# A fused attention and GEGLU kernel: weights loaded ahead of q and v of batch 1, the first GEGLU ahead of its q part, the first output projection beside batches 1 and 2, v weighted on GpSimd

## Chip, cores, metric

One core of one Trainium2 chip. The metric is the device time of one execution in microseconds; smaller is better. Runs of the kernel before and of a variant alternate on the same chip.

## The reference, cut to what matters

```python
# q, k, v: 8 batches x 8 heads x 576 x 64; omega: 128 x 64
def phi(x):                       # x is already scaled
    h = einsum('bhsd,md->bhsm', x, omega) - sum(x*x)/2
    return exp(h - max(h, over m)) / sqrt(128)
q_p, k_p = phi(q), phi(k)
kv, z = einsum('bhsm,bhsd->bhmd', k_p, v), sum(k_p, over s)
x = (q_p @ kv) / (q_p @ z + 1e-6)          # 4608 tokens x 512
out = (gelu(x @ w_gate) * (x @ w_val)) @ w_out     # d_ff = 1536
```

For each batch of attention the kernel transposes k and q, takes exp of the projected keys (k_p), their maxima (from which a weight wk for each row of v), v times wk, the products kz of keys and v, the exp of the projected queries, and the numerators and denominators (nd), whose quotient x is transposed. Nine token tiles of 512 rows then go through GEGLU (12 gates, 12 vals) and the output projection (48 matmuls each). In steady state the attention of batch t+1 runs beside the projection of tile t-1 and the GEGLU of tile t.

## The kernel before: the parts that matter

```python
att = PSUM pool, bufs=2 (two banks each);  mo = PSUM pool, bufs=4 (one bank each)
ld  = SBUF pool, bufs=2 (k_in, q_in, vf);  work = SBUF pool, bufs=2

load_kq("k", 0, parts=2); load_kq("q", 0); load_v(0)       # DMAs issued by GpSimd
load_kq("q", 1); load_kq("k", 1); load_gv(0); load_v(1)    # load_gv: 512 columns of gate and val
load_gv(1); load_gv(2); load_kq("k", 2); load_kq("q", 2)
# ... three loads of w_out, then load_v(2)

def transposed_dma(nm, b):        # used from batch 2 on; issued on the SyncE queue
    t_sb = work.tile([P, NI, P], BF16, name=f"{nm}T", tag="kqT")
    nc.sync.dma_start_transpose(out=t_sb, in_=loaded.pop((nm, b)))

def v_half(self, half):
    nc.vector.tensor_mul(ve[half], vf[half], wk[half])     # 128 x 1152
    nc.vector.tensor_copy(ve[half, D], wk[half])

def start():                      # batches 0 and 1, GEGLU 0; the issue order of each engine
    kp(0, dve); kp(1, act)        # transposed on TensorE in four pieces, copied out
    a.k_chunk(0); a.k_chunk(1); kp(2, act); kp(3, dve)
    a.k_chunk(2); a.k_chunk(3); qp(0, act); qp(1, dve)
    a.k_chunk(4); qp(2, act); qp(3, dve); a.weights()
    a.q_chunk(0); a.v_half(0); a.q_chunk(1); a.v_half(1)
    a.q_chunk(2); a.kz(0)
    # ... q chunks, nd and x of batch 0 interleaved with q of batch 1 (transposes, q chunks), k of batch 1
    g = Gated(0); g.gate(0); n.k_chunk(2); g.val(0); n.k_chunk(3); g.gate(1); n.k_chunk(4)
    n.weights(); g.gelu(0); g.mul(0); n.v_half(0); g.gelu(1); g.val(1); g.mul(1); n.v_half(1)
    for jf in range(2, 12):
        g.both(jf)                # gate, gelu, val, mul
        # jf 3: n.kz(); jf 4 to 8: n.nd; jf 5 to 9: n.xt; jf 5 and 9: transposed_dma of k and q of batch 2

def step(t, before):              # t = 1, 2, ...
    p = Projection(t - 1, before.gated); a = Attention(t + 1)
    begun = a.k_pair(0); load_batch(t + 2, begun)
    p.go(15); a.k_pair(2); p.go(13)                # go(n): n projection matmuls
    a.k_chunk(4); a.q_chunk(0); a.weights(); a.v_half(0)
    p.go(11); a.q_chunk(1); a.q_chunk(2); a.v_half(1); p.go(9)
    # ... gate 0, last q chunks, gelu 0, val 0, both(1), kz, then GEGLU with nd of the batch
```

Some names in the code: `kp(i, engine)` and `qp(i, engine)` transpose piece i of k or q on TensorE and copy it out on the engine named. `k_chunk(c)` projects one of five chunks of keys, takes its exp on ScalarE and its maxima on VectorE; `k_pair(c)` does two chunks crosswise: ScalarE begins with one and VectorE with the other. `q_chunk(c)` projects queries and takes their exp. `nd(i)` makes numerators, denominators and their quotient, `xt(i)` transposes that quotient. A PSUM buffer holds the result of matmuls until other engines have read it.

The softmax here doesn't subtract the row's maximum and nothing guards it: scores larger than these inputs give would overflow.

## Time and profile before

| kernel before | |
|---|---|
| median of the first three runs (lowest to highest) | 360.52 us (359.94 to 363.45) |
| span of the profiled execution, TensorE busy | 358.9 us, 338.2 us |
| TensorE idle from 5 to 60 us | 11.5 us (55 less the busy times of those windows) |
| TensorE idle from 60 to 340 us | 3.1 us, in part matmul records that the trace lacks (it shows 3 of the 4 of the first gate below) |

The lines below are from the overview: the span and the rows of 40 slices of about 9 us, with each digit the busy tenths of a slice. PEclk is the granted TensorE clock in tenths.

```profile
span 358.9 us, 6528 instructions
...
PE   6786997999999999999999999999999999999994
...
DVE  3986884747475747584758475757665334323431
ACT  4897324563457246623763366436643113303310
...
PEclk9899999999999999999999999999999999999999
```

The sum of busy times is in the table. TensorE is full from the eighth slice on. As long as it stays full there, relief of another engine is worth nothing; what idle time can be won lies in the first 60 us (another 4.7 us lie at the very end, after 340 us, which the change leaves alone). The next lines are windows of that stretch (start:end and length, then busy us and number of instructions for PE, PEld, DVE, ACT and POOL, and last the granted clock, the DMA share and GB/s).

```profile
core 0: us, PE busy (x) PEld busy (x) DVE busy (x) ACT busy (x) POOL busy (x), PEclk, DMA share, GB/s
10.00:15.00 5.00, 4.08 (x34) 2.43 (x34) 4.73 (x8) 4.50 (x8) 1.49 (x2) 0.66 1.11 309
15.00:20.00 5.00, 4.34 (x107) 2.95 (x107) 4.44 (x11) 4.90 (x12) 1.01 (x2) 1.00 1.22 208
20.00:25.00 5.00, 4.26 (x61) 2.84 (x59) 4.45 (x17) 4.99 (x11) 1.51 (x3) 1.00 1.19 282
...
55.00:60.00 5.00, 2.53 (x14) 0.98 (x12) 1.38 (x2) 2.45 (x3) 0.00 (x0) 1.00 1.25 146
66.00:80.00 14.00, 13.79 (x140) 6.29 (x141) 8.23 (x12) 9.20 (x17) 0.00 (x0) 1.00 1.02 257
80.00:90.00 10.00, 9.95 (x81) 5.05 (x79) 7.37 (x15) 2.99 (x5) 0.00 (x0) 1.00 0.30 61
```

ScalarE and VectorE are nearly full from 10 to 25 us, so it is they that set the pace there. From 55 to 60 TensorE is busy half of the time. The timeline of TensorE names the causes (start, duration, instruction, and in brackets the idle time before it and what ended it):

```profile
27.51 1.04 PE L325 MATMUL g_ps<-xT,w_gate_sb 128*128 128x512 bf16 x3
...
36.05 1.02 PE L325 MATMUL g_ps<-xT,w_gate_sb 128*128 128x512 bf16 x4 [2.91 <-ACT g_gelu L331]
...
60.00 0.62 PE L204 MATMUL pk<-omegaT_124,kT 64*128 64x128 bf16 x16 [2.47 <-DMA kT<-k_in]
```

GEGLU 0 starts at 27.51. Its third gate waits 2.91 us for the first GELU, which ScalarE's timeline shows behind one table load:

```profile
33.87 0.23 ACT L234 ACTIVATE wk<-nmax 128x36 f32<-128x36 f32 x1 [1.06 <-DVE nmax L214]
34.11 1.28 ACT L331 ACT_TABLE_LOAD   x1
35.40 1.09 ACT L331 ACTIVATE g_gelu<-g_ps 128x512 bf16<-128x512 f32 x2
```

The last wait, 2.47 us, is for the DMA transpose of k of batch 2. On SyncE's queue its issue alone takes 11.87 us (start, duration), and the chain of waits (the second line) gives it 18.86 us until it lands; it starts as soon as k has landed, with q and v of batch 2 and w_out still loading:

```profile
41.09 11.87 SPq L157 DMA_TRANSPOSE kT<-k_in  x1
...
41.09 18.86 DMA kT<-k_in
```

### The profile page before, as it was taken

Reading aid. Unit: us, or ns where it says so; the run is one execution under the profiler, and the core shown is the slowest. Engines: PE = TensorE matmul, PEld = TensorE weight load, DVE = VectorE, ACT = ScalarE, POOL = GpSimd, SP = SyncE. Lnnn points to the kernel's source line nnn. Section 1 sums busy time; section 2 is a strip of 40 time slices with the busy share of each in tenths; the row PEclk is TensorE's granted clock in tenths of the full one; section 3 lists DMA queues with packets and bytes.
Section 4 is the critical chain, followed back from the end, with each engine's and each line's share of the span. In section 5 each row is a group of like instructions: output and inputs, shape, how many; then the busy total and the mean of one; then the engine's idle time right before and its main releaser. Section 6 shows DMA issues by size and latency. Waiting matters only on the chain.

```text
span 358.9 us, 6528 instructions
## 1 busy us (share of the span) xinstructions
PE 338.2 (94%) x2653; PEld 164.1 (46%) x2694; DVE 207.4 (58%) x337; ACT 162.6 (45%) x260; POOL 26.1 (7%) x40
## 2 busy tenths in 40 slices
PE   6786997999999999999999999999999999999994
PEld 3552553454444544454445443544354444444443
DVE  3986884747475747584758475757665334323431
ACT  4897324563457246623763366436643113303310
POOL 8222001100020002000200020000000000000000
PEclk9899999999999999999999999999999999999999
DMA  8999999983289257944593439561312040031013
GB/s 121 270 272 208 207 214 166 220 229 66 68 148 299 58 76 114 317 63 90 85 311 82 102 50 315 115 104 29 76 22 58 21 98 0 1 74 45 0 31 90
DMA packets 64399, 44.12 MB, mean 123 GB/s; under 512 B 44784, under 2 KB 57840, under 8 KB 64368
## 3 DMA queue, kind: packets, MB, share of 16 engines
q0 software_dynamic: 15392, 23.60, 31.3%
q1 hardware_dynamic: 48816, 19.97, 26.2%
q8 instruction: 21, 0.34, 0.4%
q10 hardware_dynamic: 160, 0.13, 0.1%
q14 instruction: 10, 0.08, 0.1%
HBM read 37.78 MB, written 9.44 MB: 132 GB/s over the span
## 4 chain that ended last, share of the span: by engine, by line
PE 84%; DMA 6%; ACT 3%; DVE 3%; issue 2%; POOLq 0%
PE o_ps L386 26%; PE v_ps L338 24%; PE g_ps L325 23%; DMA kT<-k_in 5%; PE kz_ps L270 3%; PE pk L204 3%; PE nd L285 2%; PE pq L242 2%; DVE nmax L214 2%; ACT k_p L209 1%; ACT q_pT L245 1%; DMA k_in<-in_k_dram 1%; PE o_ps L374 1%; ACT kT L172 0%; ACT L331 0%
## 5 line engine op out<-in xcount | busy, mean ns | idle before, releaser
L343 DVE TENSOR_TENSOR gated<-g_gelu,v_ps 128x512 bf16<-128x512 bf16 x108 | 73.6, 687 | 100.1 <-PE v_ps L338 71.4
L331 ACT ACTIVATE g_gelu<-g_ps 128x512 bf16<-128x512 f32 x108 | 63.7, 597 | 138.5 <-PE g_ps L325 131.6
L325 PE MATMUL g_ps<-xT,w_gate_sb 128*128 128x512 bf16 x409 | 108.7, 379 | 4.0 <-ACT g_gelu L331 2.9
L338 PE MATMUL v_ps<-xT,w_val_sb 128*128 128x512 bf16 x422 | 108.9, 379 | 1.3 <-issue 1.0
L386 PE MATMUL o_ps<-w_out_sb,gated 128*128 128x512 bf16 x412 | 93.8, 379 | 1.1 <-issue 1.0
L338 PEld LDWEIGHTS <-w_val_sb 128*128 128x128 bf16 x432 | 41.6, 98 | 51.2 <-issue 1.9
L386 PEld LDWEIGHTS <-gated 128*128 128x128 bf16 x420 | 39.1, 98 | 49.3 <-issue 4.1
L325 PEld LDWEIGHTS <-w_gate_sb 128*128 128x128 bf16 x432 | 39.5, 98 | 45.8 <-issue 3.2
L214 DVE TENSOR_REDUCE nmax<-pk 128x8 f32<-128x1024 f32 (+1 forms) x40 | 43.8, 1115 | 14.6 <-ACT k_p L209 9.1
L209 ACT ACTIVATE k_p<-pk 128x1024 bf16<-128x1024 f32 (+1 forms) x40 | 36.9, 938 | 19.5 <-PE pk L204 16.1
L245 ACT ACTIVATE q_pT<-pq 128x512 bf16<-128x512 f32 (+1 forms) x80 | 38.3, 564 | 16.4 <-PE pq L242 16.3
L390 DVE COPY o_sb<-o_ps 128x512 f32<-128x512 f32 x35 | 24.1, 688 | 21.6 <-PE o_ps L386 21.0
L293 DVE TENSOR_TENSOR x_sb<-nd,iden 128x512 bf16<-128x512 f32 (+3 forms) x45 | 28.4, 630 | 1.5
L256 DVE TENSOR_TENSOR v_ext<-vf,wk 128x1152 bf16<-128x1152 f32 x16 | 21.7, 1357 | 2.4 <-ACT wk L234 2.4
L84 POOL DMA_DIRECT2D k_in<-in_k_dram x9 | 6.8, 755 | 170.8 <-ACT k_p L209 167.6
L285 PEld LDWEIGHTS <-q_pT 128*128 128x128 bf16 (+1 forms) x320 | 13.9, 100 | 9.9 <-DVE x_sb L293 2.8
L204 PE MATMUL pk<-omegaT_124,kT 64*128 64x128 bf16 x288 | 13.3, 219 | 5.0 <-DMA kT<-k_in 2.5
L285 PE MATMUL nd<-kz,q_pT 128*128 128x65 bf16 (+1 forms) x320 | 16.1, 194 | 0.7 <-ACT kT L172 0.4
L204 PEld LDWEIGHTS <-kT 64*128 64x128 bf16 x288 | 8.7, 94 | 14.9 <-issue 10.8
L242 PE MATMUL pq<-qT,omegaT_124 64*128 64x512 bf16 (+1 forms) x80 | 12.8, 365 | 1.0 <-ACT q_pT L245 0.8
L270 PEld LDWEIGHTS <-k_p 64*128 64x128 bf16 x576 | 9.8, 94 | 3.5 <-issue 3.4
L270 PE MATMUL kz_ps<-v_ext,k_p 64*128 64x65 bf16 x576 | 10.8, 191 | 0.3 <-DVE v_ext L258 0.2
(40 smaller groups left out, 104.0 us busy)
## 6 DMA issues: line engine op xcount, KB each, us to landing
vf<-in_v_dram POOLq DMA_DIRECT2D x8, 1152.0 KB, 12.7
out_dram<-o_sb SPq DMA_DIRECT2D x70, 128.0 KB, 3.6
q_in<-in_q_dram POOLq DMA_DIRECT2D x8, 576.0 KB, 10.0
k_in<-in_k_dram POOLq DMA_DIRECT2D x7, 576.0 KB, 6.2
w_gate_sb<-in_moe_w_gate_dram POOLq DMA_DIRECT2D x3, 512.0 KB, 21.8
w_val_sb<-in_moe_w_val_dram POOLq DMA_DIRECT2D x3, 512.0 KB, 21.5
w_out_sb<-in_moe_w_out_dram POOLq DMA_DIRECT2D x3, 512.0 KB, 22.3
k_in<-in_k_dram POOLq DMA_DIRECT2D x2, 288.0 KB, 4.6
```

Of the source, the lines that this page charges most:

```text
L204: nc.tensor.matmul(pk[:, a, i, :], self.kT[sl, i0 + i, :], omegaT2[sl])
L209: return nc.scalar.activation(self.k_p[:, :, i0:i0 + n, :], pk[:, :, :n, :], func=Exp)
L214: nc.vector.reduce_max(self.nmax[:, :, i0:i0 + n], pk[:, :, :n, :], axis=AX, negate=True)
L245: nc.scalar.activation(dst[:, a, i0:i0 + n], pq[:, a, :n, :].rearrange("m i (e p) -> m i e p", e=2), func=Exp)
L270: nc.tensor.matmul(kz_ps[e][:, j * DP1:(j + 1) * DP1], self.k_p[sl, u % 2, u // 2, :], self.ve[sl, u, :], start=(r == 0), stop=(r == R - 1))
L285: nc.tensor.matmul(nd[h // 4][:n, (h % 4) * DP1:(h % 4 + 1) * DP1], self.q_pT[:, e, u:u + nr, :].rearrange("m r p -> m (r p)"), self.kz_sb ...
L293: nc.vector.tensor_mul(x_sb[:n].rearrange("p (g h d) -> p g h d", g=2, h=4)[:, gs], ndv[:, :, :, :D], iden[:n, gs].broadcast_to((n, gs.sto ...
L325: nc.tensor.matmul(g_ps, w_gate_sb[:, jm, fs], self.xT[:, jm, :], start=(jm == 0), stop=(jm == N_DM - 1))
L331: nc.scalar.activation(g_gelu, self.ps[jf], func=Gelu)
L338: nc.tensor.matmul(v_ps, w_val_sb[:, jm, fs], self.xT[:, jm, :], start=(jm == 0), stop=(jm == N_DM - 1))
L343: nc.vector.tensor_mul(self.gated[:, jf, :], self.gelus[jf], self.vps[jf])
L386: nc.tensor.matmul(self.o_ps, self.gated[:, jf, qq * P:(qq + 1) * P], w_out_sb[:, jf, :], start=(jf == 0), stop=(jf == N_DFF - 1))
```

## The change

The intent: have gate and val weights in place early, let GEGLU 0 start before anything of batch 1 but its keys, give the first projection the q part of batch 1 (and batch 2's keys) to run beside, and relieve VectorE of v. The core of the diff, with cuts marked; `k_first` and `k_second` are `k_pair` cut in two. Not shown: nd of batch 0 now uses the att buffers of PSUM, and the transposes of x of batch 1 the mo buffers.

```diff
+    load_kq("k", 1); load_gv(0); load_kq("q", 1)
+    load_gv(1); load_gv(2); load_v(1)        # then w_out; batch 2 from load_batch(2, None) below
 def start():
         kp(0, dve)
         kp(1, act)
-        a.k_chunk(0); a.k_chunk(1); kp(2, act); kp(3, dve); ... (as above)
+        a.k_pair(0)
+        kp(2, dve)
+        kp(3, act)
+        a.k_pair(2)
+        p4 = a.k_proj(4)
+        a.k_max(*p4)
+        a.weights()
+        a.k_exp(*p4)
+        qp(0, act); qp(1, dve); a.q_chunk(0); qp(2, dve); a.q_chunk(1); qp(3, dve)
+        a.v_half(0, nc.vector)
+        a.q_chunk(2); a.kz(0); a.v_half(1, nc.vector); a.q_chunk(3); a.kz(1); a.q_chunk(4)
         ... nd and x of batch 0 (x copies now on ScalarE), k of batch 1, no q of batch 1
+        begun, pair = n.k_first(0); g.gate(0); n.k_second(pair); g.val(0)
+        begun, pair = n.k_first(2); g.gate(1); n.k_second(pair); g.val(1)
+        n.k_chunk(4)
+        a.nd(4)
+        g.gelu(0)
+        g.mul(0)
+        a.xt(4, dve)
+        n.weights()
+        g.gelu(1)
+        g.mul(1)
+        load_batch(2, None)
+        n.v_half(0, nc.gpsimd); n.v_half(1, nc.gpsimd)
         for jf in range(2, N_DFF):
             g.both(jf)
+            # jf 2 to 5: qp of batch 1; jf 9: transposed_dma("k", 2); jf 10: n.kz()
+    def second(before, n):                 # in place of step(1)
+        p = Projection(0, before.gated)
+        for c in range(5):
+            n.q_chunk(c)
+            p.go(4 if c < 3 else 5)
+        a = Attention(2); a.kT = kqT.pop(("k", 2))
+        n.nd(0); n.nd(1); n.xt(0, dve)
+        begun, pair = a.k_first(0)
+        load_batch(3, begun)
+        p.go(2); n.xt(1, dve); a.k_second(pair); n.nd(2)
+        p.go(2); n.nd(3); n.xt(2, dve)
+        begun, pair = a.k_first(2)
+        a.qT = transposed_dma("q", 2)
+        p.go(2); n.xt(3, dve); a.k_second(pair); n.nd(4)
+        p.go(3); n.xt(4, dve); a.k_chunk(4)
+        p.go(3); a.q_chunk(0); a.weights()
+        a.v_half(0, nc.gpsimd); a.v_half(1, nc.gpsimd)
+        p.go(4); a.q_chunk(1); a.q_chunk(2); p.go(48 - p.done)
+        ... gate 0, last q chunks, then GEGLU 1 as before
 def step(t, before):                       # t = 2, 3, ...
-        a.v_half(0); ... a.v_half(1)
+        a.v_half(0, nc.gpsimd)
+        a.v_half(1, nc.gpsimd)
```

More of the change, by code (lines that the diff above doesn't have):

```diff
@@ L111 @@
     load_v(0)
-    load_kq("q", 1)
     load_kq("k", 1)
     load_gv(0)
-    load_v(1)
+    load_kq("q", 1)
     load_gv(1)
     load_gv(2)
-    load_kq("k", 2)
-    load_kq("q", 2)
+    load_v(1)
     for c in range(3):
         nc.gpsimd.dma_start(out=w_out_sb[:, 4 * c:4 * c + 4, :], in_=wo[:, 4 * c:4 * c + 4, :])
-    load_v(2)
     still = singles.tile([P, T_TOK], BF16)
@@ L187, in __init__, with two_banks @@
             self.xs = {}
-        def two_banks(self, name):
-            if self.b == 0:
+        def two_banks(self, name, halves=False):
+            if halves:
                 halves = [mo_tile([P, 512], F32, name) for _ in range(2)]
@@ L221, in k_chunk, with k_first @@
             self.k_max(*p)
-        def k_pair(self, c):
+        def k_first(self, c):
             p0, p1 = self.k_proj(c), self.k_proj(c + 1)
@@ L228, in k_pair, with k_second @@
             self.k_max(*p1)
-            self.k_exp(*p1)
-            self.k_max(*p0)
+            return begun, (p0, p1)
+        def k_second(self, pair):
+            self.k_exp(*pair[1])
+            self.k_max(*pair[0])
+        def k_pair(self, c):
+            begun, pair = self.k_first(c)
+            self.k_second(pair)
             return begun
@@ L247, in q_chunk, with v_half @@
                                      func=Exp)
-        def v_half(self, half):
+        def v_half(self, half, eng):
             vf = loaded["v", self.b]
@@ L255, in v_half @@
             isl = slice(half * NI // 2, (half + 1) * NI // 2)
-            nc.vector.tensor_mul(vev[:, isl, :, :D], vfv[:, isl],
+            eng.tensor_mul(vev[:, isl, :, :D], vfv[:, isl],
                                  wkv[:, isl].unsqueeze(3).broadcast_to((P, NI // 2, 2, D)))
-            nc.vector.tensor_copy(vev[:, isl, :, D], wkv[:, isl])
+            eng.tensor_copy(vev[:, isl, :, D], wkv[:, isl])
         def kz(self, half=None):
             if half != 1:
-                self.kz_ps = self.two_banks("kz_ps")
+                self.kz_ps = self.two_banks("kz_ps", halves=half is not None)
             kz_ps, groups = self.kz_ps
@@ L300, in nd, with xt @@
                     out=dst, in_=x_sb[o:o + m, :]))
-        def xt(self, i):
+        def xt(self, i, copy):
             r0 = 2 * i
@@ L306, in xt @@
             x_sb = self.xs[i]
-            xt_ps = (mo_tile if self.b == 0 else att_tile)([P, N_DM, P], BF16, "xt_ps")
+            xt_ps = mo_tile([P, N_DM, P], BF16, "xt_ps")
             for c in range(N_DM):
@@ L311, in xt @@
             put_x(self.b * S + r0 * SP, n,
-                  lambda dst, o, m: nc.vector.tensor_copy(dst, xt_ps[:, :, o:o + m]))
+                  lambda dst, o, m: copy(dst, xt_ps[:, :, o:o + m]))
     class Gated:
@@ L398, in load_batch @@
         for dma in load_kq("k", b) + load_kq("q", b) + load_v(b):
+            if begun is None:
+                continue
             tc.add_manual_dep(dma.ins, begun.ins.name, mybir.DependencyInfo(
                 mybir.DependencyClass.Sync, mybir.DependencyReason.DATA))
+    act, dve = nc.scalar.copy, nc.vector.tensor_copy
     def start():
-        act, dve = nc.scalar.copy, nc.vector.tensor_copy
         a = Attention(0)
@@ L408, in start @@
         a.qT, qp = transposed_pe("q", 0)
+        n = Attention(1)
         kp(0, dve)
         kp(1, act)
-        a.k_chunk(0)
-        a.k_chunk(1)
-        kp(2, act)
-        kp(3, dve)
-        a.k_chunk(2)
-        a.k_chunk(3)
+        a.k_pair(0)
[6 more added lines that the diff above has]
+        a.k_exp(*p4)
         qp(0, act)
         qp(1, dve)
-        a.k_chunk(4)
-        qp(2, act)
+        a.q_chunk(0)
@@ L421, in start @@
+        qp(2, dve)
+        a.q_chunk(1)
         qp(3, dve)
-        a.weights()
-        a.q_chunk(0)
-        a.v_half(0)
-        a.q_chunk(1)
-        a.v_half(1)
+        a.v_half(0, nc.vector)
         a.q_chunk(2)
         a.kz(0)
-        n = Attention(1)
-        n.qT, qp = transposed_pe("q", 1)
-        n.kT, kp = transposed_pe("k", 1)
+        a.v_half(1, nc.vector)
         a.q_chunk(3)
-        qp(0, dve)
-        qp(1, dve)
         a.kz(1)
         a.q_chunk(4)
-        n.q_chunk(0)
+        n.kT, kp = transposed_pe("k", 1)
@@ L438, in start @@
+        n.qT, qp = transposed_pe("q", 1)
+        kp(0, act)
         a.nd(0)
-        n.q_chunk(1)
-        qp(2, act)
         a.nd(1)
-        a.xt(0)
-        qp(3, act)
-        n.q_chunk(2)
+        a.xt(0, act)
+        kp(1, act)
         a.nd(2)
-        a.xt(1)
-        kp(0, act)
-        n.q_chunk(3)
+        a.xt(1, act)
         a.nd(3)
-        a.xt(2)
-        kp(1, act)
-        n.q_chunk(4)
-        a.nd(4)
-        a.xt(3)
-        kp(2, act)
-        a.xt(4)
-        n.k_chunk(0)
@@ L458, in start @@
-        kp(3, act)
-        n.k_chunk(1)
+        a.xt(2, act)
+        kp(2, dve)
+        begun, pair = n.k_first(0)
+        a.xt(3, act)
+        kp(3, dve)
         g = Gated(0)
         g.gate(0)
-        n.k_chunk(2)
+        n.k_second(pair)
         g.val(0)
-        n.k_chunk(3)
+        begun, pair = n.k_first(2)
         g.gate(1)
+        n.k_second(pair)
+        g.val(1)
         n.k_chunk(4)
-        n.weights()
+        a.nd(4)
         g.gelu(0)
         g.mul(0)
-        n.v_half(0)
+        a.xt(4, dve)
@@ L471, in start @@
+        n.weights()
         g.gelu(1)
-        g.val(1)
         g.mul(1)
-        n.v_half(1)
+        load_batch(2, None)
+        n.v_half(0, nc.gpsimd)
+        n.v_half(1, nc.gpsimd)
         for jf in range(2, N_DFF):
             g.both(jf)
-            if jf == 3:
-                n.kz()
-            if 4 <= jf < 9:
-                n.nd(jf - 4)
-            if 5 <= jf < 10:
-                n.xt(jf - 5)
-            if jf == 5:
-                kqT["k", 2] = transposed_dma("k", 2)
-            if jf == 9:
-                kqT["q", 2] = transposed_dma("q", 2)
+            if 2 <= jf < 6:
+                qp(jf - 2, dve)
+            if jf == 9:
+                kqT["k", 2] = transposed_dma("k", 2)
+            if jf == 10:
+                n.kz()
@@ new lines, in start @@
+        return g, n
+    def second(before, n):
[3 more added lines that the diff above has]
+            p.go(4 if c < 3 else 5)
+        a = Attention(2)
+        a.kT = kqT.pop(("k", 2))
+        n.nd(0)
+        n.nd(1)
+        n.xt(0, dve)
+        begun, pair = a.k_first(0)
+        load_batch(3, begun)
+        p.go(2)
+        n.xt(1, dve)
+        a.k_second(pair)
+        n.nd(2)
+        p.go(2)
+        n.nd(3)
+        n.xt(2, dve)
+        begun, pair = a.k_first(2)
+        a.qT = transposed_dma("q", 2)
+        p.go(2)
+        n.xt(3, dve)
+        a.k_second(pair)
+        n.nd(4)
+        p.go(3)
+        n.xt(4, dve)
+        a.k_chunk(4)
+        p.go(3)
+        a.q_chunk(0)
+        a.weights()
+        a.v_half(0, nc.gpsimd)
+        a.v_half(1, nc.gpsimd)
+        p.go(4)
+        a.q_chunk(1)
+        a.q_chunk(2)
+        p.go(48 - p.done)
+        g = Gated(1)
+        g.gate(0)
+        a.q_chunk(3)
+        a.q_chunk(4)
+        return gates(g, a, 3)
@@ L487, in start, with gates @@
+    def gates(g, a, nxt):
+        g.gelu(0)
+        g.val(0)
+        g.mul(0)
+        g.both(1)
+        a.kz()
+        if nxt < B:
+            kqT["k", nxt] = transposed_dma("k", nxt)
+        for jf in range(2, N_DFF):
+            g.both(jf)
+            if jf == 2:
+                a.nd(0)
+            if jf < 6:
+                a.nd(jf - 1)
+            if jf == 5 and nxt < B:
+                kqT["q", nxt] = transposed_dma("q", nxt)
         return g
@@ L509, in step @@
         a.weights()
-        a.v_half(0)
+        a.v_half(0, nc.gpsimd)
+        a.v_half(1, nc.gpsimd)
         p.go(11)
@@ L513, in step @@
         a.q_chunk(2)
-        a.v_half(1)
         p.go(9)
@@ L519, in step @@
         a.q_chunk(4)
-        g.gelu(0)
-        g.val(0)
-        g.mul(0)
-        g.both(1)
-        a.kz()
-        if t + 2 < B:
-            kqT["k", t + 2] = transposed_dma("k", t + 2)
-        for jf in range(2, N_DFF):
-            g.both(jf)
-            if jf == 2:
-                a.nd(0)
-            if jf < 6:
-                a.nd(jf - 1)
-            if jf == 5 and t + 2 < B:
-                kqT["q", t + 2] = transposed_dma("q", t + 2)
-        return g
+        return gates(g, a, t + 2)
     E = mybir.EngineType
-    with tc.manual_schedule(engines={E.Activation, E.PE, E.DVE, E.SP}):
-        g = start()
-        for t in range(1, N_TOK):
+    with tc.manual_schedule(engines={E.Activation, E.PE, E.DVE, E.SP, E.Pool}):
+        g, n = start()
+        g = second(g, n)
+        for t in range(2, N_TOK):
             g = step(t, g)
```

## The prediction

> **What bounds it.** The overview gives TensorE 338.2 of 358.9 us. In 5-us windows it is idle about 13 us of the first 60 and 5 at the end; from 60 to 340 it is 98-99% busy. So only the start can change. The timeline and chain of waits show what holds it there: ScalarE (4.2 to 5 of every 5 us from 10 to 30) and VectorE, not weights. GEGLU 0 starts at 27.5 when x of batch 0 is ready; its third gate waits 2.9 us for the first GELU. The first gate weights, issued at 6.2, land 15.6 later, about 22: not the limit. Last, k of batch 2, landed at 41.1, needs 18.9 us for its DMA transpose among other loads; TensorE waits 2.5 us for it, until 60.0.
>
> **What changes.** Weights come 3 us earlier: worth nothing, since x is later. The q part of batch 1 (TensorE: q chunks 2.0 us, nd 1.2, transposes of x 1.0) moves from places where TensorE was idle or GEGLU covered VectorE to the projection after it.
>
> Stages, added up by program order with durations from the trace (exp 1.03, max 1.23, copies 0.4-0.7, q exps 1.1 a chunk):
> - Keys of batch 0: pairing exp and max saves 0.6 us, but the third transposed piece is copied behind them, chunk 4 waits for a PSUM buffer, and q is transposed only after it. First q exp about 16.7, not 14.2. VectorE weights v after all q copies: first numerators near 22.5, not 18.7. Less work follows: GEGLU 0 starts near 29 (27.5).
> - The key weights of batch 1 (Exp) stand between GELU 0 and 1: two more table switches, 1.28 us each in the trace; the Trainium skill, "ScalarE: Activation LUTs", section "What ACT_TABLE_LOAD costs", has the same 1283 ns. TensorE's third val starts near 40 (36.9).
> - The rest of GEGLU 0 loses nd and transposes of x, gains transposes of q: ends near 60 (57.5, then the 2.5 wait). At 60 both kernels stand at the same place, but the new one has 4.2 us of batch 1 left.
> - Projection 0: VectorE has five nd evictions (0.85 each), five x copies, five maxima (5.5) and output copies, about 13 us, while TensorE has 6-7 there; with two attention PSUM buffers it waits some 6 us. Table load and q exps add 0.5. The DMA transpose of q of batch 2 now collides with batch 3's loads: 0 to 3 us.
> - v on GpSimd: the Trainium skill, "GPSIMD Engine Reference", section 3.1, has 4497 ns for a two-input op of 2048 elements; my estimate from it for 1152 is 2.5 us, 5.5 for both halves with copies (VectorE: 1.36 a half). Between wk (69.4) and kz (76.9) are 7.5 us: it hides. VectorE's relief is worth nothing, TensorE bounds these stages.
>
> **Sum.** 4.2 moved, about 7 of new waits: 11 us on the path, nothing given back. 360.5 + 11 = 371.5, say 371 us, 8 in 10 between 364 and 377. Faster by over 2%: 0.05; within: 0.2; slower: 0.75.
>
> **Right if.** Timeline: GEGLU 0 at 29 +-1.5; extra table loads around the first GELUs; TensorE 6 us or more idle in the first projection, waiting for maxima and x_sb; the second GEGLU's first val near 85 (74.4); later steps 36.9 us each; no wait of kz on GpSimd.
>
> **Wrong if.** First numerators no later than before, no table reload for the weights, or maxima and evictions overlapping more in the projection: about 363. GpSimd over 3.5 us a half: a wait in each of seven steps, over 380. DMA contention on transposes: towards 377.

## The result, and the profile after

The changed kernel takes 380.72 us (median of 4 runs, 380.22 to 381.12) against 361.05 us (4 runs) of the kernel before. The ratio is 1.0529, with a 95% interval of 1.0481 to 1.0576. A ratio is the mean time of one kernel's runs over that of the other's of the same rounds, so it is not quite the ratio of the medians quoted. All outputs are right. It is slower by over 5%: the direction of the prediction is right, and the time lies 3.7 us above its range.

The overview of the changed kernel, the same lines:

```profile
span 378.4 us, 6565 instructions
...
PE   6586999637999999999999999999999999999995
...
DVE  4567442741556365727472747283727424323422
ACT  4657536323535643664367337724763303302310
...
PEclk9659899887999999999999999999999999999999
```

There is a new hole in the ninth and tenth slices (76 to 95 us), where DVE and ACT are empty too, and PEclk is low in several early slices. The windows, in the same columns:

```profile
10.00:15.00 5.00, 1.97 (x27) 1.48 (x28) 3.47 (x4) 3.01 (x5) 1.49 (x2) 0.69 1.10 314
15.00:20.00 5.00, 3.23 (x30) 1.48 (x30) 2.73 (x5) 3.58 (x7) 1.18 (x2) 0.50 1.24 206
20.00:25.00 5.00, 4.42 (x95) 3.71 (x90) 2.99 (x8) 2.44 (x5) 1.05 (x2) 0.50 1.23 208
...
66.00:80.00 14.00, 9.51 (x112) 5.60 (x111) 11.18 (x21) 4.92 (x7) 2.31 (x3) 0.88 0.73 124
80.00:90.00 10.00, 3.04 (x11) 0.68 (x10) 1.38 (x2) 1.58 (x4) 0.61 (x1) 0.68 0.79 175
```

Three things are to be seen. From 10 to 20 us TensorE is busy 5.2 us where it was 8.4, and its clock stays at 0.50 until about 28. From 66 to 80 it is busy 9.51 of 14 us, not 13.79, while VectorE has 11.18. From 80 to 90 it is busy 3.04 of 10. The timeline of TensorE:

```profile
22.89 1.16 PE L290 MATMUL nd<-kz,q_pT 128*128 128x65 bf16 x16
...
30.41 1.02 PE L330 MATMUL g_ps<-xT,w_gate_sb 128*128 128x512 bf16 x4 [0.70 <-ACT xT L317]
...
38.10 0.27 PE L314 MATMUL xt_ps<-ident,x_sb 64*128 64x64 bf16 x4 [2.22 <-ACT g_gelu L336]
...
87.45 0.61 PE L247 MATMUL pq<-qT,omegaT 64*128 64x512 bf16 x2 [6.96 <-DMA qT<-q_in]
...
94.16 1.04 PE L343 MATMUL v_ps<-xT,w_val_sb 128*128 128x512 bf16 x4
```

The first numerators start at 22.89, as predicted (22.5), and GEGLU 0 at 30.41 (27.51 before). The 6.96 us at 87.45 are one wait, for the DMA transpose of q of batch 2. The second GEGLU's first val starts at 94.16; 85 was predicted. The chain of waits has this one piece in the hole, until the transpose lands at 87.40:

```profile
72.72 14.68 DMA qT<-q_in
```

The transpose is issued on SyncE's queue at 72.72, and its issue alone takes 9.46 us:

```profile
72.72 9.46 SPq L154 DMA_TRANSPOSE qT<-q_in  x1
```

GpSimd had issued the three loads of batch 3 in the 2.3 us just before it. The lines below show the first and the last of the three, and the first v multiplication on GpSimd for batch 2, 2.15 us:

```profile
70.46 0.81 POOL L84 DMA_DIRECT2D k_in<-in_k_dram  x1 [26.16 <-ACT k_p L206]
...
71.99 0.78 POOL L91 DMA_DIRECT2D vf<-in_v_dram  x1
89.39 2.15 POOL L261 TENSOR_TENSOR v_ext<-vf,wk 128x1152 bf16<-128x1152 f32 x1 [16.62 <-ACT wk L239]
```

ScalarE around the first GELUs, with the three table loads that were predicted:

```profile
36.16 1.28 ACT L336 ACT_TABLE_LOAD   x1
37.46 0.60 ACT L336 ACTIVATE g_gelu<-g_ps 128x512 bf16<-128x512 f32 x1
38.07 1.28 ACT L239 ACT_TABLE_LOAD   x1
39.37 0.23 ACT L239 ACTIVATE wk<-nmax 128x36 f32<-128x36 f32 x1
39.62 1.28 ACT L336 ACT_TABLE_LOAD   x1
40.91 1.08 ACT L336 ACTIVATE g_gelu<-g_ps 128x512 bf16<-128x512 f32 x2
```

From 95 us on the steps take as long as before: the table loads ahead of two successive key exps stand at 116.80 and 153.75, 36.95 us apart, as before (96.80 and 133.75).

### The profile page after: what moved, and what is told of

It is laid out like the page before. It is cut to its first block, busy times and chain, and to the rows that moved or that the text cites. A ratio compares the mean times of both kernels' runs of the same rounds, so it can differ in the third digit from the quotient of the medians.

```text
span 378.4 us, 6565 instructions
## 1 busy us (share of the span) xinstructions
PE 349.9 (92%) x2694; PEld 168.3 (44%) x2694; DVE 188.2 (50%) x300; ACT 165.3 (44%) x261; POOL 58.7 (16%) x68
## 4 chain that ended last, share of the span: by engine, by line
PE 88%; DVE 4%; DMA 4%; ACT 2%; issue 0%
PE g_ps L330 25%; PE v_ps L343 25%; PE o_ps L391 24%; DMA qT<-q_in 4%; PE pq L247 3%; PE kz_ps L275 3%; PE pk L201 3%; PE nd L290 2%; DVE nmax L211 2%; ACT k_p L206 1%; PE warm_ps L126 1%; DVE x_sb L298 1%; PE o_ps L379 1%; PE qT_ps L168 1%; PE kT_ps L168 1%
## 5 line engine op out<-in xcount | busy, mean ns | idle before, releaser
L330 PE MATMUL g_ps<-xT,w_gate_sb 128*128 128x512 bf16 x432 | 111.6, 381 | 1.2 <-ACT xT L317 0.7
L343 PE MATMUL v_ps<-xT,w_val_sb 128*128 128x512 bf16 x432 | 111.8, 382 | 0.0
L391 PE MATMUL o_ps<-w_out_sb,gated 128*128 128x512 bf16 x420 | 98.0, 383 | 0.0
L261 POOL TENSOR_TENSOR v_ext<-vf,wk 128x1152 bf16<-128x1152 f32 x14 | 30.1, 2149 | 72.6 <-ACT wk L239 68.0
L298 DVE TENSOR_TENSOR x_sb<-nd,iden 128x512 bf16<-128x512 f32 (+1 forms) x40 | 27.6, 690 | 1.4
L247 PE MATMUL pq<-qT,omegaT 64*128 64x512 bf16 (+1 forms) x80 | 14.1, 398 | 8.0 <-DMA qT<-q_in 7.0
L201 PE MATMUL pk<-omegaT,kT 64*128 64x128 bf16 x288 | 13.5, 228 | 5.0 <-ACT k_p L206 4.2
L275 PEld LDWEIGHTS <-k_p 64*128 64x128 bf16 x576 | 10.8, 99 | 5.1 <-issue 5.1
L275 PE MATMUL kz_ps<-v_ext,k_p 64*128 64x65 bf16 x576 | 11.7, 197 | 1.4 <-DVE v_ext L263 1.4
```

Of the source, the lines that this page charges most:

```text
L201: nc.tensor.matmul(pk[:, a, i, :], self.kT[sl, i0 + i, :], omegaT2[sl])
L275: nc.tensor.matmul(kz_ps[e][:, j * DP1:(j + 1) * DP1], self.k_p[sl, u % 2, u // 2, :], self.ve[sl, u, :], start=(r == 0), stop=(r == R - 1))
L298: nc.vector.tensor_mul(x_sb[:n].rearrange("p (g h d) -> p g h d", g=2, h=4)[:, gs], ndv[:, :, :, :D], iden[:n, gs].broadcast_to((n, gs.sto ...
L330: nc.tensor.matmul(g_ps, w_gate_sb[:, jm, fs], self.xT[:, jm, :], start=(jm == 0), stop=(jm == N_DM - 1))
L343: nc.tensor.matmul(v_ps, w_val_sb[:, jm, fs], self.xT[:, jm, :], start=(jm == 0), stop=(jm == N_DM - 1))
L391: nc.tensor.matmul(self.o_ps, self.gated[:, jf, qq * P:(qq + 1) * P], w_out_sb[:, jf, :], start=(jf == 0), stop=(jf == N_DFF - 1))
```

## The experiments

The runs were made in three sets, on different chips, where the median of the kernel before was 361.50, 362.03 and 361.76 us. So a difference between variants of different sets is uncertain by some tenths of a us: by ratios, the 3.4 us of a5_keys would be 3.8, and the 3.2 us of c2_spread 3.5.

### Loads of batch 3 held (a1_hold)

The transpose of q keeps its place and its time of issue; the loads that were issued just before it come after the last key exp instead.

```diff
         begun, pair = a.k_first(0)
-        load_batch(3, begun)
...
-        a.k_chunk(4)
+        p4 = a.k_proj(4)
+        load_batch(3, a.k_exp(*p4))
+        a.k_max(*p4)
```

> The changed kernel, with the loads of batch 3 held until the last key exp of batch 2 (about 80 us); the DMA transpose of q of batch 2 is still issued where it was, at about 72.7 us. Theory, collision: the transpose took 14.7 us because three loads were issued in the 2.3 us before it; alone it lands in 4 to 6 us, before its use at about 79.8, so the 7.0 us wait goes, and with it most of the half-clock stretch behind it (about 1.3 us): 372 us, ratio to the kernel before 1.03. Rival, lateness: it is issued too late whatever the traffic: no more than 2 us gained, 379. Rival, other engine: VectorE or ScalarE would hold TensorE there anyway: no gain, 381.

Measured: 371.3 us, ratio 1.0269 (1.0227 to 1.0311), that is 9.4 us less than the changed kernel. SyncE's queue and TensorE's timeline of this run (from a profiled execution with a span of 370.1 us; a second one, of 371.2 us, has the same: issued at 72.93 in 1.96 us, landed after 4.1):

```profile
72.71 1.93 SPq L154 DMA_TRANSPOSE qT<-q_in  x1
```

```profile
80.41 0.39 PE L247 MATMUL pq<-qT,omegaT 64*128 64x512 bf16 x2
...
85.86 1.04 PE L343 MATMUL v_ps<-xT,w_val_sb 128*128 128x512 bf16 x4
```

The issue comes at the same time, 72.71, but takes 1.93 us, and the transpose lands 4.0 us after it began, not 14.7. TensorE takes the first q chunk at 80.41 without a wait. The two profiled spans differ by 8.3 us: 7.0 of the first q chunk's start and 1.3 between it and the first val (6.7 us in the changed kernel, where the clock had fallen to 0.50 in the wait and came back at about 90; 5.45 here), the price of a TensorE that had stood idle.

### Transpose issued early (a2_early)

```diff
             p.go(4 if c < 3 else 5)
         a = Attention(2)
         a.kT = kqT.pop(("k", 2))
+        a.qT = transposed_dma("q", 2)
...
         begun, pair = a.k_first(2)
-        a.qT = transposed_dma("q", 2)
```

> The changed kernel, with the DMA transpose of q of batch 2 put in program order right behind the last q chunk of batch 1, so that it is issued at about 66 us, ahead of the loads of batch 3 (70.5 us) and of the second output store. Collision and lateness both: it lands at about 71 us, no wait, 372 us (ratio 1.03). Other engine: 381. Together with the held loads it tells collision (both gain 8 to 9 us) from lateness (only this one gains).

Measured: 372.3 us, ratio 1.0289 (1.0254 to 1.0325). It is issued at 66.42 and lands after 4.0 us. Both mends work, and lateness alone is refuted by the first. In this run the batch's loads land 6.4 (k), 9.1 (q) and 11.1 us (v) after their issue; in the changed kernel, with the transpose beside them, 6.5, 10.4 and 14.0. So the loads delayed the transpose by 10.7 us, the transpose the last load by 2.9.

### Key weights ahead of the first GELU (a3_weights)

```diff
         n.k_chunk(4)
+        n.weights()
         a.nd(4)
         g.gelu(0)
         g.mul(0)
         a.xt(4, dve)
-        n.weights()
```

> The changed kernel, with the key weights of batch 1 ahead of the first GELU again: one table load there, not three. My stage sum gave the two extra switches about 2 us of TensorE (third val near 40 instead of 38): 378.5 to 379.5 us. Rival: they cost nothing, because gate 2 waits for the last x piece and its PSUM buffer anyway, and the weights first delay the first GELU by 1.5 us: 380.7 plus or minus 0.5, or slower by up to 1.

Measured: 381.95 us, ratio 1.0557 (1.0519 to 1.0595): the rival was right, though 1.2 us of loss is a little more than its "up to 1". ScalarE has one table load, and the wait for it is where it was, longer:

```profile
36.52 1.28 ACT L336 ACT_TABLE_LOAD   x1
```

```profile
38.47 0.37 PE L314 MATMUL xt_ps<-ident,x_sb 64*128 64x64 bf16 x4 [3.21 <-ACT g_gelu L336]
```

The transpose of x waits 3.21 us for the first GELU instead of 2.22, because the weights now keep that GELU waiting for the last maximum. The run does two things at once, it saves two table loads and delays the first GELU; what the loads cost in the changed kernel is seen in its own profile: there TensorE is never idle between the third gate, at 38.83, and the second GELU. The first GELU, not the second, is what TensorE waits for.

### TensorE kept busy in its early waits (a4_fill)

```diff
+    def fill(n):
+        fill_ps = mo_tile([P, T_TOK], F32, "fill_ps")
+        for _ in range(n):
+            nc.tensor.matmul(fill_ps, still[:, :P], still)
...
         a.k_pair(0); kp(2, dve); kp(3, act)
+        fill(5)
         a.k_pair(2)
+        fill(9)
         p4 = a.k_proj(4)
...
+        fill(3)        # ahead of a.q_chunk(0)
+        fill(5)        # ahead of a.kz(0)
```

> The changed kernel, with 22 matmuls of zeros on TensorE in its waits between 9 and 20 us, so that it is not idle there. Theory: idle TensorE is what halves its clock from 12 to 28 us (0.50 in the windows), and the halved clock is the 1.4 us by which GEGLU 0 started later than I had summed (30.4, not 29): the clock stays near 1.0 from 15 us on, GEGLU 0 starts at 29 to 29.5, 379.3 us (-1.0 to -1.5). Rival: the chain there runs over ScalarE and VectorE and the clock costs nothing: 380.7. If the clock follows time and not idleness it stays at 0.50 and nothing changes.

Measured: 377.37 us, ratio 1.0434 (1.0394 to 1.0475), 3.3 us less than the changed kernel, more than I had put on it. Its windows (same columns) and GEGLU 0's first gate:

```profile
10.00:15.00 5.00, 4.44 (x43) 2.26 (x42) 3.39 (x4) 2.78 (x5) 1.29 (x2) 1.00 1.11 310
15.00:20.00 5.00, 3.98 (x58) 2.05 (x58) 3.40 (x5) 3.63 (x8) 1.14 (x3) 1.00 1.24 207
20.00:25.00 5.00, 3.55 (x87) 2.81 (x86) 3.49 (x10) 3.56 (x8) 1.30 (x2) 1.00 1.23 207
```

```profile
27.80 1.02 PE L330 MATMUL g_ps<-xT,w_gate_sb 128*128 128x512 bf16 x4 [0.81 <-ACT xT L317]
```

The clock is 1.00 from 10 to 30 us, and GEGLU 0 starts at 27.80, 2.6 us sooner than in the profile of the changed kernel (1.7 sooner than in that of a7_loads, whose clock had recovered earlier), though no wait for another engine was taken away. So keeping TensorE from idling did keep the clock up here, and the clock lay on the path: kz, nd and the transposes of x alternate with VectorE and ScalarE, and each took longer. In the changed kernel the 36 kz matmuls took 1.17 us, here 0.76. The fill did not help later: behind the 2.22 us wait for the first GELU the clock is 0.50 from 35 to 40 us.

### Batch 0 in the order of before (a5_keys)

On top of the held loads.

```diff
-        a.k_pair(0); kp(2, dve); kp(3, act); a.k_pair(2)
-        p4 = a.k_proj(4); a.k_max(*p4); a.weights(); a.k_exp(*p4)
-        qp(0, act); qp(1, dve); a.q_chunk(0); qp(2, dve); a.q_chunk(1); qp(3, dve); a.v_half(0, nc.vector) ...
+        a.k_chunk(0); a.k_chunk(1); kp(2, act); kp(3, dve); a.k_chunk(2); a.k_chunk(3)
+        qp(0, act); qp(1, dve); a.k_chunk(4); qp(2, act); qp(3, dve); a.weights()
+        a.q_chunk(0); a.v_half(0, nc.vector); a.q_chunk(1); a.v_half(1, nc.vector) ...
```

> The changed kernel with the loads of batch 3 held (as in the run that held them, 371.3 us), and with the keys, q and v of batch 0 in the order of the kernel before (no pairing, q transposed among the keys, both v halves early). My stage sum has the new order 4.2 us late at the first numerators and 1.7 late at GEGLU 0, and the trace 3.0 late there with the halved clock: first numerators near 19 us, GEGLU 0 at 26.5 to 27.5, 367.5 to 368.5 us (ratio 1.018). Rival, the pairing helps and the lateness comes from the clock alone: no gain, 371.

Measured: 367.91 us, ratio 1.0165 (1.0131 to 1.0200), 3.4 us less than with the loads held alone. The first numerators and GEGLU 0's first gate:

```profile
19.67 1.15 PE L290 MATMUL nd<-kz,q_pT 128*128 128x65 bf16 x16
...
26.92 1.02 PE L330 MATMUL g_ps<-xT,w_gate_sb 128*128 128x512 bf16 x4 [0.82 <-ACT xT L317]
```

They start at 19.67 (22.89 in the changed kernel) and 26.92 (30.41), although the clock was still 0.50 from 15 to 20 us and 0.52 from 20 to 25. So the order of batch 0 itself costs most of this; it may also be that less idle time brings the clock back sooner (it is 1.00 from 25 to 30, against 0.61 in the changed kernel), which the run does not separate.

### Projection matmuls spread (c2_spread)

On top of the early transpose.

```diff
         for c in range(5):
             n.q_chunk(c)
-            p.go(4 if c < 3 else 5)
+            p.go(4 if c == 0 else 3)
...
+        # go(4), go(5), go(4), go(4), go(5), go(5), go(5) between nd, xt and keys,
+        # where go(2), go(2), go(2), go(3), go(3) stood;
+        # load_batch(3, begun) now behind a.k_first(2), not a.k_first(0)
...
+        a.q_chunk(0); ...; g.gate(0); a.q_chunk(1); g.val(0); a.q_chunk(2)
+        g.gate(1); a.q_chunk(3); a.q_chunk(4); g.val(1)
```

> The changed kernel with the early transpose of q of batch 2 (372.3 us), and with the projection matmuls spread: 16, not 22, beside the q chunks of batch 1, 32, not 12, through the stretch where VectorE evicts numerators and takes maxima, the first two gates and vals beside the q chunks of batch 2. Theory: VectorE's 13 us there stay, but TensorE has as much to do: its waits between 66 and 80 us shrink from about 6 us to about 1: 367 us (ratio 1.017). Rival, the PSUM buffers and the order of dependences hold TensorE, not a lack of work: at most 1 us gained, 371.5.

Measured: 369.13 us, ratio 1.0191 (1.0163 to 1.0219), 3.2 us less than with the early transpose alone, between theory and rival. The windows from 66 to 80 us, of the early transpose and then of this run:

```profile
66.00:80.00 14.00, 9.90 (x111) 5.56 (x110) 10.96 (x20) 4.75 (x6) 2.31 (x3) 0.79 0.90 173
```

```profile
66.00:80.00 14.00, 12.63 (x135) 6.80 (x133) 12.79 (x24) 5.49 (x8) 2.30 (x3) 1.00 0.59 112
```

TensorE is busy 12.63 of 14 us instead of 9.90 and the clock is 1.00, so lack of work and the low clock that came of it were most of what held it there. (The loads of batch 3 also come later in this run; they are not the cause, since holding them alone, in a1_hold, left TensorE at 9.51 of these 14 us.) The kz of batch 2 starts 4.9 us sooner (84.62 against 89.56), but 1.2 us of this are given back at once (the next gate starts 2.46 us after kz begins, not 1.27): with the gates moved ahead, the next gate waits 0.77 us for a GELU and half of kz 0.18 us for v on GpSimd.

### Order of loads as before (a7_loads)

On top of the held loads.

```diff
+    load_kq("q", 1)
     load_kq("k", 1); load_gv(0)
-    load_kq("q", 1)
+    load_v(1)
     load_gv(1); load_gv(2)
-    load_v(1)
```

> The changed kernel with the loads of batch 3 held (371.3 us) and with the order of loads of batch 1, gate and val weights as before the change (q and v of batch 1 ahead of most weights). Theory: GEGLU 0 waits for x, not for weights, in both orders (its first gate weights land near 22 us, its start is near 30): 371.3 plus or minus 1, no wait of a gate or val on a weight load. Rival, the earlier weights are worth something: their 2.5 to 3 us show, 373.5 or more.

Measured: 372.56 us, ratio 1.0310 (1.0264 to 1.0355), against 371.3 us and 1.0269 with the changed order: 1.3 us more, just outside the "plus or minus 1", but the intervals overlap. No gate or val waits for a load in its profile, and GEGLU 0 starts at 29.50, behind the copy of x on ScalarE. No worth of the earlier weights is shown.

### The kernel before with v on GpSimd (b1_gps)

```diff
+            eng = nc.gpsimd if self.b > 0 else nc.vector
-            nc.vector.tensor_mul(...)
+            eng.tensor_mul(...)          # and the copy; both halves right behind the weights
```

> The kernel before with one part of the change: v of batches 1 to 7 weighted on GpSimd, both halves right behind the weights. Theory: 2.15 us a half and 4.7 us for both fit into the 7.5 us before kz, VectorE's relief is worth nothing since TensorE bounds these stages: 361, ratio 0.997 to 1.003. Rival: VectorE's relief or GpSimd's use of memory moves it by over 0.5%.

Measured: 361.79 us, ratio 0.9982 (0.9954 to 1.0010). It neither helps nor harms; in the profile no kz waits for GpSimd.

### The kernel before with v of batch 2 late (b3_vlate)

```diff
-    load_v(2)
...
         for jf in range(2, N_DFF):
-            g.both(jf)
+            begun = g.both(jf)
+            if jf == 9:
+                # load_v(2), depending on this GELU
```

> The kernel before, with the load of v of batch 2 held until the tenth GELU (about 53 us), so that it does not share the DMA engines with the transpose of k of batch 2. Theory, as for q in the changed kernel: without 1.15 MB beside it that transpose lands about 3.5 us sooner than 59.9 and TensorE's 2.5 us wait before the first projection goes: 358.8, ratio 0.993. Rival: the wait is not made by shared engines: 361.

Measured: 360.84 us, ratio 0.9961 (0.9926 to 0.9995). The transpose of k of batch 2 takes 15.8 us instead of 18.9. TensorE does not wait for it in this profile, but that proves little: GEGLU 0 started late there, at 29.76, and TensorE came to the keys of batch 2 at 61.08, when a transpose of 18.9 us from 40.8 would have landed too. The gain is less than the 2.5 us hoped for, about 1.4 by the ratio. Three of its six runs had a mean clock of 0.989 and took 359.09 to 359.91 us, the others, the profiled one among them, 0.975 to 0.979 and 361.77 to 362.57: in that profile the clock is 0.50 from 15 to 20 us, where it is 1.00 in the profile shown of the kernel before. So the start of both kernels comes in two forms, and a gain of 1 us is best read between runs of the same clock: the three runs at 0.989 average 359.58 us, the five runs of the kernel before at 0.988 or 0.989, of all three sets, 360.43 (a sixth, at 0.990, took 362.58). So the late load gives about 0.9 us, on few runs.

### The kernel before with TensorE kept busy (b4_fill)

```diff
         kp(2, act); kp(3, dve)
+        fill(3)
         a.k_chunk(2)
+        fill(2)
         a.k_chunk(3)
...
+        fill(3)        # ahead of a.q_chunk(2)
```

> The kernel before with 8 matmuls of zeros in TensorE's waits between 8 and 15 us. Theory: its clock, 0.50 from about 11 to 14 us in the trace shown and longer in some runs, stays at 1.0; the start there runs mostly over ScalarE and VectorE, so 0.5 to 2 us: 359 to 361, ratio 0.995 to 0.999. Rival, the fill stands in the way of real work: slower.

Measured: 361.22 us, ratio 0.9988 (0.9953 to 1.0023), which can't be told from no change. In its profile the clock is 1.00 from 10 to 30 us, but then falls behind the 2.91 us wait for the first GELU: it is 0.66 from 35 to 40, and the third gate takes 1.75 us, where in the profile shown of the kernel before the same wait left the clock at 1.00 and the gate took 1.02. Its six runs lie between 360.72 and 361.79 with clocks of 0.992 to 0.995. The kernel before, in the same rounds, lies between 360.05 and 363.26, and its runs at the lowest clock (0.976) are the five of 363.0 us or more.

### The kernel before with all three (x_best)

The edits of the last three runs together.

> The kernel before with what helped or did no harm to it: v of batch 2 loaded late, v of batches 1 to 7 on GpSimd, the same 8 matmuls. If the effects add up, about 359 us, ratio 0.992 to 0.996; if they overlap, 361.

Measured: 359.61 us, ratio 0.9950 (0.9914 to 0.9986): half a per cent faster than the kernel before, the best version. Part of this is that none of its runs has the low clock: five of the eleven runs of the kernel before do (363.0 us or more), and the other six average 360.71, against 359.89 here.

### The changed kernel with all mends (y_all)

The early transpose, the order of batch 0 as before, the spread projection, and the fill of the kernel before.

> The changed kernel with all mends that worked: early transpose of q of batch 2, batch 0 in the order of before, projection matmuls spread, and 8 matmuls of zeros in TensorE's early waits. If the effects add up (9.4 of the collision, 3.4 of the order, 3.2 of the spread, about 1 of the clock): 364 us, ratio 1.006. What is then left against the kernel before is the q part of batch 1 that was moved (4.2 us by my sum) less the 2.5 us wait for k of batch 2 that it spares. Rival, the mends overlap: 367 or more.

Measured: 363.67 us, ratio 1.0066 (1.0013 to 1.0120). The effects add up as expected, and the change so mended is still slower than the kernel before.

## Why the prediction was wrong, point by point

**The step that failed** is this term of the sum: "The DMA transpose of q of batch 2 now collides with batch 3's loads: 0 to 3 us." The mechanism was named rightly, its size was not, and the sum of 371 counted it as next to nothing (some 6 us of other waits and 0.5 already make its "about 7"). It measured 7.0 us of waiting and 1.3 us of halved clock behind it, more than even the prediction's "DMA contention on transposes: towards 377" allowed; with the collision taken away, the kernel takes 371.3 us (loads held) or 372.3 us (transpose early), where I had 371. In my working, I had let the transpose be issued at about 71.5 and share the engines evenly with loads begun at 68.7. In the trace the loads were issued from 70.46 to 72.77, the transpose at 72.72, and it landed at 87.40, 1.4 us after the last of the loads (71.99 plus 14.0). The kernel before had shown the same: its transpose of k took 18.86 us among loads. I read that as a wait of 2.5 us, not as the rate at which a transpose makes way.

The other points:

- *GEGLU 0 near 29.* It started at 30.41. The order of batch 0 costs 3.4 us (a5_keys), more than the 1.5 (27.5 to 29) that I gave it, and none of it was in the sum, in which both kernels stood at the same place at 60. What I had left out is the halved clock: keeping TensorE busy starts GEGLU 0 at 27.80.
- *Three table loads.* They are there, 1.28 us each, and they cost nothing that a3_weights could find. My stage came out right (third val at 40.19, predicted 40) by luck, because errors offset each other: GEGLU 0 started 1.4 us later than I had it and the third gate took 1.57 us at a halved clock, while the 2 us that I gave the loads never reached TensorE.
- *End of GEGLU 0 near 60.* The next work starts at 60.24. Right.
- *Some 6 us of waits in the projection, for VectorE.* TensorE was idle 4.5 of the 14 us from 66 to 80 in the changed kernel. Of the waits, the profile puts 1.6 us down to x_sb on VectorE and 2.6 to key exps on ScalarE, of which each had itself waited for a maximum on VectorE. Spreading the matmuls gained 3.2 us in the end, after 1.2 were given back. Right in kind, a little too large.
- *GpSimd hides.* Right: 2.15 us a half (2.5 estimated), 4.6 for both, no difference in time.
- *Weights early are worth nothing.* No gain shown.
- *Moved work, 4.2 us.* Not isolated by a run. With the collision, the order, the waits and the clock mended, 363.67 us is left against 361.76: 1.9 us. My sum for that remainder is 4.2 less the 2.5 us wait for k that the change spares, 1.7 us. That agrees. So does the kernel before with its own mends: x_best, of the same rounds, has no such wait in its profile and takes 359.61, so that 4.1 us are left against it. But no run takes the move alone, and the term itself is argued and not shown.

So the 19.7 us come, by the runs, from the collision (8.4 to 9.4), the order of batch 0 (3.4), the unspread projection (3.2), a rest of about 2 put down to the clock (y_all lies 2 us below the sum of the other mends; the fill alone had gained 3.3), and about 2 that stay. How the DMA engines divide their time between a transpose and loads stays open: the issue of the transpose took 9.46 us among loads and 1.93 alone, which points to its being held back as it is issued, but no run tells this from an uneven division later.

## What to carry to other kernels

Before you move a DMA transpose, look in the trace for what else is issued within some microseconds of it, and cost it by the slowest case that the trace already shows, not by its time alone. When work is moved beside a projection, add up each engine for that stretch by itself: TensorE needs as much work there as the slowest other engine has, or it waits and then runs slowly. A relieved engine, or weights that come sooner, are worth nothing where neither was waited for.

## What the Trainium skill lacked or had wrong

- "DMA: Bandwidth & Descriptors", section "Queues, rings and completion order", says that an engine goes round its queues packet by packet. It gives no figure for a DMA transpose among loads. Here 4.0 us became 14.7 beside three loads, and 18.9 beside the five still queued in the kernel before, while the last of the three loads went only from 11.1 to 14.0.
- "TensorE: Matmul & The Clock Gate", in its table of why this matters, asks for no idle gap over about 3 us. In the changed kernel the clock fell at about 12 us within a wait of 2.37 us, and stayed at 0.50 until 28 us although TensorE was busy 88% of 20 to 25. Filler matmuls, 8 or 22, kept it at 1.00 from 10 to 30. Nor does the length of one gap decide: the same wait for the first GELU, 2.91 or 2.92 us, left the clock at 1.00 in the kernel before and in b1_gps, and was followed by 0.50 in b4_fill and x_best.
- "ScalarE: Activation LUTs", section "What ACT_TABLE_LOAD costs", adds a drain of about 1380 ns to the load's 1283. Here a load takes 1.28 us and the next instruction starts 0.02 us after it, right behind the GELU before: no drain shows.
- "GPSIMD Engine Reference", section 3.1, has GpSimd 1.96 times slower than VectorE on a two-input op. For v (float32 in, bfloat16 out, the weight broadcast, 1152 elements) it is 2.15 against 1.35 us in these profiles, 1.6 times.
